# Attention then FFN on one core: FFN-only steps between the first two batches, range data sent once per batch, FFN spans that follow the attention chunks

## The chip, the core and the metric

One core of one Trainium2 chip runs one launch of the kernel. The metric is the device time of that launch in microseconds (us); less is better. The engines are named as the profile names them: PE (TensorE matmul), PEld (its weight load), DVE (VectorE), ACT (ScalarE), POOL (GpSimd), and SP, which here only issues transfers. SPq, ACTq and POOLq are the engines' instruction queues. Each engine works through its own instructions strictly in the order in which the program gives them, so an instruction that waits holds back all that stand behind it on that engine.

## What is computed

```python
def _attn_ref(q, k, v, beacon_k, beacon_v):          # q, k, v: (8, 8, 576, 64)
    k_all = np.concatenate([beacon_k, k], axis=2)     # 16 beacon rows in front: 592
    v_all = np.concatenate([beacon_v, v], axis=2)
    scores = scale * np.matmul(q, k_all.transpose(0, 1, 3, 2))
    scores = np.where(causal, -1e9, scores)           # beacons are always seen
    a = np.exp(scores - scores.max(-1, keepdims=True))
    a /= a.sum(-1, keepdims=True) + 1e-09
    return np.matmul(a, v_all)

def reference(**inputs):
    x = attn_out.transpose(0, 2, 1, 3).reshape(8 * 576, 512)
    return (np.maximum(x @ w_gate, 0) * (x @ w_val)) @ w_out   # 512 -> 1536 -> 512
```

## The kernel before, in words

Attention of 8 batches and 8 heads fills a matrix xT (512 x 4608, bf16, on chip); the FFN reads xT in tiles of 512 tokens. Both are cut into small pieces that a hand-written loop interleaves.

**Attention.** Heads go in 4 pairs per batch. A pair has 4 steps (i = 0 to 3), so a batch has 16. A step is `qk` (scores into PSUM tile s, 2 buffers), `softmax` (one exp on ACT, L270, then one or two masks on POOL, L273) and `av` (L293). Chunk 0 (tokens 0 to 240) is step 0; chunk 1 (240 to 496) is steps 1 and 2; chunk 2 (496 to 576) is step 3. At the last step of a chunk, `av` lets DVE take the reciprocal of the sums (L300, tile r) and multiply into xT (L302), and SP sends two rows of r to rsum (L304). At the end `count_in_range` looks at rsum on DVE (L348 to L352) and counts with one matmul (L354); every engine reads the count, and a general path that is not taken here hangs on it.

**FFN.** A group is either an up (L320 to L328: 4 matmuls with wg, relu on ACT, 4 matmuls with wv, a product on DVE into hT) or a down (L333: 12 matmuls, a copy on ACT, one store by SP). A whole tile is 12 ups and 4 downs. Ups and downs share the PSUM tile f (2 buffers).

**The loop.** It goes over a list of steps, two at a time; call one turn a pass. A pass issues `qk` of its two steps, then twice (softmax of one step, one FFN group from a queue if it holds any), then `av` of the two steps of the pass before. FFN groups come into the queue when the tokens of a span are ready; a span is a range of tokens. Spans before: 0 to 240, 240 to 512, then whole tiles. Batch 0 takes its steps chunk by chunk over all pairs; later batches take (1, 2) of each pair, then (0, 3) of each pair.

**Loading.** Batch 0 loads q and k as four wide tiles each and turns them on PE (L390 to L396, `turn_pair`, `turn_tail`). Each later batch has 15 units of 128 rows (k, q, v in turn, five row tiles t = 0 to 4). A unit is loaded by SP (L220) into one of the `stage` buffers (8), cast to bf16 by POOL (L238) and, for k and q, turned by a transfer that SP issues (L243) out of one of 6 `half` buffers. `fetch` puts the unit's load, cast and turn at steps of the batch before. In front of a pass's `qk` all that is due is issued: so POOL meets the casts of the next batch between the masks of the current one. The weights are loaded by POOL (L248): 8 quarters of wg and wv and one wo.

Of the kernel before, what the change touches and what calls it, by code (L numbers as in the profile page):

```python
# [146 lines left out]
def kernel(  # L147
# [38 lines left out]
    rsum = const.tile([2 * B * NP, S], FP32, name="rsum")  # L186
# [15 lines left out]
    class Batch:  # L202
        def __init__(self, b):
            self.b = b
            self.qT = kvq.tile([P, NP, S], BF16, name="qT")
            self.kT = kvq.tile([P, NP, NKT * P], BF16, name="kT")
            self.v = kvq.tile([P, NKT, d_model], BF16, name="v")
            self.raw, self.h = {}, {}
            nc.gpsimd.memset(self.kT[:, :, Stot:], 0.0)
# [69 lines left out]
    def av(pr, i):  # L279
# [18 lines left out]
        if i == last:  # L298
            r = nrm.tile([P, 256], FP32, name="r")
            nc.vector.reciprocal(r[:, :cn], o[:, 1, :cn])  # L300
            t0 = pr.batch.b * S + cq0
            nc.vector.tensor_mul(xT[:, pr.p, t0:t0 + cn], o[:, 0, :cn], r[:, :cn])  # L302
# [41 lines left out]
    def count_in_range():  # L344

        rows = 2 * B * NP
        ge = const.tile([rows, S], FP32, name="ge")
# [19 lines left out]
    with tc.manual_schedule():  # L367
# [5 lines left out]
        start = main.enter_context(tc.tile_pool(name="start", bufs=1))  # L373
# [3 lines left out]
        def load_pair(x, src, p, eng):  # L377
            t = wide[x, p] = start.tile([P, 2, 4 * D], FP32, name=f"wide_{x}{p}")
            eng.dma_start(t, src[0, 2 * p:2 * p + 2, :WIDE].rearrange("h (p r) d -> p h (r d)", r=4))

        def load_tail(x, src, beacon, eng):
            t = tails[x] = start.tile([P, d_model], FP32, name=f"tail_{x}")
# [5 lines left out]
        def turn_pair(x, p, copy):  # L388
            h = half.tile([P, 4, P], BF16, name="half")
            copy(h.rearrange("x r (h d) -> x h r d", d=D),  # L390
                 wide[x, p].rearrange("x h (r d) -> x h r d", d=D))
# [22 lines left out]
        load_tail("k", k, beacon_k[0], nc.sync)  # L414
        load_pair("q", q, 1, nc.scalar)
# [17 lines left out]
        for w in weights[:2]:  # L433
# [3 lines left out]
        later = {}  # L437
# [4 lines left out]
        for p in (2, 3):  # L442
            at(p - 1, lambda p=p: turn_pair("k", p, nc.vector.tensor_copy))
            at(p - 1, lambda p=p: turn_pair("q", p, nc.scalar.copy))
        at(3, lambda: turn_tail("q", nc.vector.tensor_copy))
        for t in range(2, NKT):
            at(t - 1, lambda t=t: b0.cast("v", t, nc.gpsimd.tensor_copy))
        for j, w in enumerate(weights[2:]):
            at(j // 2, w)

        def fetch(b, s0):
            at(s0, lambda: batches.append(Batch(b)))
            for j, u in enumerate(UNITS):
                s = s0 + j * 3 // 4
                at(s, lambda u=u: batches[b].load(*u))
                at(s + 2, lambda u=u: batches[b].cast(*u, nc.gpsimd.tensor_copy))
                if u[0] != "v":
                    at(s + 3, lambda u=u: batches[b].turn(*u))

        work, ready = [], {}  # L460
        for b in range(B):


            if b == 0:
                for c, (c0, cn, first, last) in enumerate(CHUNKS):
                    work += [(b, p, i) for p in range(NP) for i in range(first, last + 1)]
# [5 lines left out]
            if b + 1 < B:  # L472
                fetch(b + 1, 16 * b + (1 if b else 3))
# [67 lines left out]
```

## Time and profile before

| | |
|---|---|
| runs | 462.07 and 462.93 us, median 462.5 |
| the profiled execution | 461.52 us, of which the span from first to last instruction is 459.8 us |
| PE busy | 405.0 us (88%), 3545 matmuls |
| DVE, ACT, POOL busy | 243.9, 196.0 and 132.0 us |
| mean granted clock of PE | 0.967 of full speed |
| moved by DMA | 52.20 MB, mean 114 GB/s |

A row of a timeline has the start and the length in us, the engine, the line, the operation, what it writes <- what it reads, and in brackets how long the engine idled before it and what released it. PEclk is the granted clock of PE: 1.00 is 2.4 GHz, 0.50 is 1.2 GHz. MB in the DMA views agrees with packets times bytes in units of 2^20 bytes.

### The profile page before, as it was taken

How to read it: one execution, taken by the hardware profiler on the slowest of the kernel's cores; microseconds unless marked ns; L12 is line 12 of the kernel's file. 1: busy time of each engine (PE TensorE's matmuls, PEld its weight loads, DVE VectorE, ACT ScalarE, POOL GpSimd, SP SyncE). 2: the span in 40 equal slices, each digit the busy share in tenths (PEclk: the TensorE clock that was granted, in tenths of full speed). 3: DMA queues.
4: the chain of work that ended last, by engine and by line, in shares of the span. 5: the costliest groups of instructions: out<-in, count | busy, mean ns of one | idle time of the engine just before them, and what ended most of it. 6: DMA issues, size and time to landing. Idle time of an engine off the chain costs nothing.

```text
span 459.8 us, 9167 instructions
## 1 busy us (share of the span) xinstructions
PE 405.0 (88%) x3545; PEld 212.4 (46%) x3545; DVE 243.9 (53%) x330; ACT 196.0 (43%) x293; POOL 132.0 (29%) x293
## 2 busy tenths in 40 slices
PE   2547569869999999999999999999999997899994
PEld 1334345655454455544544554454545543344441
DVE  2544244655677466656755775577556755221320
ACT  2623235524554455445445554465355422122321
POOL 0931344242335224512442253234312100000000
PEclk9998699979999999999999999999999999799998
DMA  9999965893495449545944793568310010002002
GB/s 208 219 191 191 203 137 118 168 148 86 113 189 118 136 94 189 110 127 123 183 93 123 125 193 98 136 123 171 88 47 1 2 69 26 1 1 93 0 24 75
DMA packets 155011, 52.20 MB, mean 114 GB/s; under 512 B 142544, under 2 KB 150352, under 8 KB 154960
## 3 DMA queue, kind: packets, MB, share of 16 engines
q1 hardware_dynamic: 147568, 45.63, 48.3%
q0 software_dynamic: 5776, 4.72, 6.4%
q10 hardware_dynamic: 1616, 1.18, 1.0%
q8 instruction: 30, 0.49, 0.5%
q14 instruction: 21, 0.17, 0.1%
HBM read 38.27 MB, written 9.44 MB: 104 GB/s over the span
## 4 chain that ended last, share of the span: by engine, by line
PE 68%; DMA 13%; DVE 8%; SPq 3%; issue 3%; ACT 2%; POOL 1%; ACTq 0%; DVEq 0%; POOLq 0%
PE f L333 21%; PE f L326 18%; PE f L320 16%; PE o L293 8%; DMA raw<-in_v_dram 6%; DVE r L300 5%; PE s L262 4%; DMA raw<-in_k_dram 2%; SPq L243 2%; DMA raw<-in_q_dram 1%; ACT e L270 1%; DMA wide_k_131<-in_k_dram 1%; SPq L220 1%; DMA wide_q_120<-in_q_dram 1%; DVE hT L328 1%
## 5 line engine op out<-in xcount | busy, mean ns | idle before, releaser
L300 DVE RECIPROCAL r<-o 128x240 f32<-128x240 f32 (+2 forms) x96 | 129.9, 1353 | 71.4 <-PE o L293 63.9
L270 ACT ACTIVATE e<-s 128x736 bf16<-128x736 f32 (+3 forms) x128 | 110.1, 863 | 108.7 <-PE s L262 106.8
L328 DVE TENSOR_TENSOR hT<-g,f 128x512 bf16<-128x512 f32 (+2 forms) x120 | 75.9, 633 | 112.7 <-PE f L326 107.8
L320 PE MATMUL f<-xT,wg 128*128 128x512 bf16 (+2 forms) x480 | 120.7, 374 | 11.1 <-DVE xT L302 9.4
L326 PE MATMUL f<-xT,wv 128*128 128x512 bf16 (+2 forms) x480 | 117.0, 368 | 6.2 <-ACT g L323 3.3
L323 ACT ACTIVATE g<-f 128x512 f32<-128x512 f32 (+2 forms) x120 | 66.5, 554 | 72.5 <-PE f L320 71.4
L333 PE MATMUL f<-wo,hT 128*128 128x512 bf16 x432 | 96.2, 379 | 0.0
L326 PEld LDWEIGHTS <-wv 128*128 128x128 bf16 x480 | 48.3, 101 | 76.4 <-issue 36.9
L273 POOL TENSOR_SCALAR_AFFINE_SELECT e<-e 128x256 bf16<-128x256 bf16 (+2 forms) x160 | 57.3, 387 | 88.6 <-ACT e L270 88.6
L293 PE MATMUL o<-e,v 128*64 128x80 bf16 (+4 forms) x704 | 58.8, 241 | 13.6 <-POOL e L273 13.6
L238 POOL CAST half<-raw 128x512 bf16<-128x512 f32 (+1 forms) x70 | 42.7, 611 | 94.9 <-DMA raw<-in_q_dram 59.0
L320 PEld LDWEIGHTS <-wg 128*128 128x128 bf16 x480 | 44.8, 102 | 48.5 <-issue 8.8
L333 PEld LDWEIGHTS <-hT 128*128 128x128 bf16 x432 | 41.1, 98 | 49.2 <-issue 1.3
L293 PEld LDWEIGHTS <-v 128*64 128x64 bf16 (+1 forms) x704 | 37.5, 113 | 39.6 <-issue 37.4
L293 PE MATMUL o<-e,ones 128*64 128x80 bf16 (+4 forms) x704 | 53.7, 236 | 0.0
L336 ACT COPY ob<-f 128x512 f32<-128x512 f32 x36 | 21.1, 585 | 65.5 <-PE f L333 56.5
L238 POOL CAST v<-raw 128x512 bf16<-128x512 f32 (+1 forms) x40 | 24.6, 615 | 56.8 <-DMA raw<-in_v_dram 54.4
L262 PE MATMUL s<-qT,kT 64*128 64x80 bf16 (+3 forms) x704 | 37.1, 239 | 2.6 <-DMA rsum<-r 2.6
L293 PEld LDWEIGHTS <-ones 128*64 128x64 bf16 (+1 forms) x704 | 36.1, 114 | 0.1
L302 DVE TENSOR_TENSOR xT<-o,r 128x240 bf16<-128x240 f32 (+2 forms) x96 | 34.3, 358 | 3.3
L262 PEld LDWEIGHTS <-kT 64*128 64x128 bf16 x704 | 22.8, 98 | 9.6 <-issue 4.1
L394 PE MATMUL f<-ident,half 128*128 128x128 bf16 x32 | 4.5, 309 | 10.2 <-DVE half L390 9.2
(36 smaller groups left out, 30.1 us busy)
## 6 DMA issues: line engine op xcount, KB each, us to landing
out_dram<-ob SPq DMA_DIRECT2D x36, 256.0 KB
raw<-in_q_dram SPq DMA_DIRECT2D x28, 256.0 KB
raw<-in_v_dram SPq DMA_DIRECT2D x24, 256.0 KB
raw<-in_k_dram SPq DMA_DIRECT2D x21, 256.0 KB
raw<-in_v_dram SPq DMA_DIRECT2D x8, 224.0 KB
raw<-in_k_dram SPq DMA_DIRECT2D x7, 224.0 KB
wg<-in_moe_w_gate_dram POOLq DMA_DIRECT2D x4, 384.0 KB, 11.8
wv<-in_moe_w_val_dram POOLq DMA_DIRECT2D x4, 384.0 KB, 13.7
```

The costliest lines, as they stand in the source:

```text
L238: copy(dst, self.raw[x, t][:n])
L262: nc.tensor.matmul(s[:, a, c:c + n], pr.batch.kT[rows, pr.p, kt * P:(kt + 1) * P], pr.batch.qT[rows, pr.p, q0:q0 + n], start=True, stop=True)
L270: nc.scalar.activation(e[:, :, :n], pr.s[i][:, :, :n], AF.Exp, scale=scale)
L273: nc.gpsimd.affine_select(out=e[:, :, c:c + m], in_=e[:, :, c:c + m], pattern=[[0, 2], [1, m]], compare_op=ALU.is_ge, fill=0.0, base=base, ...
L293: nc.tensor.matmul(o[rows, part, q0 - cq0:q0 - cq0 + n], w, e[:kr, a, c:c + n], start=(i == first and j == 0 and part == 0), stop=(i == la ...
L300: nc.vector.reciprocal(r[:, :cn], o[:, 1, :cn])
L302: nc.vector.tensor_mul(xT[:, pr.p, t0:t0 + cn], o[:, 0, :cn], r[:, :cn])
L320: nc.tensor.matmul(g[:, :n], wg[:, ki, nf * P:(nf + 1) * P], x[:, ki], start=(ki == 0), stop=(ki == KM - 1))
L323: nc.scalar.activation(gs[:, :n], g[:, :n], AF.Relu)
L326: nc.tensor.matmul(u[:, :n], wv[:, ki, nf * P:(nf + 1) * P], x[:, ki], start=(ki == 0), stop=(ki == KM - 1))
L328: nc.vector.tensor_mul(self.h[:, nf, c0:c1], gs[:, :n], u[:, :n])
L333: nc.tensor.matmul(o, self.h[:, nf, ms * P:(ms + 1) * P], wo[:, nf, :], start=(nf == 0), stop=(nf == NF - 1))
```

## The change

It does five things. (1) Between the 16 steps of batch 0 and those of batch 1 stand 8 empty steps: a pass over them issues no attention, but goes on taking FFN groups from the queue. (2) The 15 loads of batch 1 are given out from step 6 on, its casts and turns only from step 16 on, that is in the empty steps; batches 2 to 7 keep the old spacing, one step earlier. (3) Batch 1 also goes chunk by chunk, and the second tile's span is cut at token 816, where batch 1's chunk 0 ends, so that tile has 12 ups of 304 columns and 12 of 208 instead of 12 of 512. (4) r becomes one tile per batch (128 x 4 x 576), and SP sends its two rows once per batch; rsum is 16 x 2304 instead of 64 x 576. (5) In the start, q pairs 2 and 3 and the q tail are loaded by SP instead of ACT, all staging goes through the `stage` buffers (11 of them), and the order of the weights and turns is new. What is issued at a step is split in two: `ahead` before `qk`, `later` between the two `qk` and the softmax.

```diff
-    rsum = const.tile([2 * B * NP, S], FP32, name="rsum")
+    rsum = const.tile([2 * B, NP * S], FP32, name="rsum")
...
-    stage = main.enter_context(tc.tile_pool(name="stage", bufs=8))
+    stage = main.enter_context(tc.tile_pool(name="stage", bufs=11))
...
-    nrm = main.enter_context(tc.tile_pool(name="nrm", bufs=3))
+    nrm = main.enter_context(tc.tile_pool(name="nrm", bufs=2))
...
+            self.r = nrm.tile([P, NP, S], FP32, name="r")
...
-            r = nrm.tile([P, 256], FP32, name="r")
-            nc.vector.reciprocal(r[:, :cn], o[:, 1, :cn])
...
-            g = 2 * (pr.batch.b * NP + pr.p)
-            nc.sync.dma_start(rsum[g:g + 2, cq0:cq0 + cn],
-                              r.rearrange("(a x) n -> a x n", a=2)[:, 0, :cn])
+            batch = pr.batch
+            r = batch.r[:, pr.p, cq0:cq0 + cn]
+            nc.vector.reciprocal(r, o[:, 1, :cn])
...
+            batch.chunks += 1
+            if batch.chunks == NP * len(CHUNKS):
+                nc.sync.dma_start(
+                    rsum[2 * batch.b:2 * batch.b + 2],
+                    batch.r.rearrange("(a x) p s -> a x (p s)", a=2)[:, 0])
...
-        rows = 2 * B * NP
-        ge = const.tile([rows, S], FP32, name="ge")
+        rows = 2 * B
+        ge = nrm.tile([rows, NP * S], FP32, name="r")
...
-        load_pair("k", k, 1, nc.sync)
-        for p in (2, 3):
-            load_pair("q", q, p, nc.scalar)
-        load_tail("q", q, None, nc.scalar)
         for t in range(2):
             b0.load("v", t)
         for p in (2, 3):
             load_pair("k", k, p, nc.sync)
+            load_pair("q", q, p, nc.sync)
+        load_tail("q", q, None, nc.sync)
...
-        for w in weights[:2]:
+        for w in weights[:4]:
             w()
...
+        ahead[2] = [lambda x=x, p=p, c=c: turn_pair(x, p, c) for p in (2, 3)
+                    for x, c in (("k", nc.vector.tensor_copy), ("q", nc.scalar.copy))]
+        ahead[4] = [lambda: turn_tail("q", nc.vector.tensor_copy)]
+        for w in weights[4:6]:
+            at(2, w)
+        at(2, lambda: b0.cast("v", 2, nc.gpsimd.tensor_copy))
+        for w in weights[6:]:
+            at(4, w)
+        for t in (3, 4):
+            at(4, lambda t=t: b0.cast("v", t, nc.gpsimd.tensor_copy))
...
+        GAP = 8
...
-            if b == 0:
+            if b < 2:
...
+            if b == 0:
+                work += [None] * GAP
+        fetch(1, lambda j: 6 + j // 2, lambda j: 16 + j // 2, lambda j: 16 + j // 2)
+        for b in range(2, B):
+            s0 = 16 * (b - 1) + GAP
+            fetch(b, lambda j, s0=s0: s0 + j * 3 // 4, lambda j, s0=s0: s0 + 2 + j * 3 // 4,
+                  lambda j, s0=s0: s0 + 3 + j * 3 // 4)
...
-        spans = [(0, 240), (240, 512)] + [(m, m + M_TILE) for m in range(M_TILE, n_tokens, M_TILE)]
+        spans = [(0, 240), (240, 512), (512, 816), (816, 1024)]
+        spans += [(m, m + M_TILE) for m in range(1024, n_tokens, M_TILE)]
```

POOL, late in batch 0: `e` is a mask, `half` and `v` are casts of batch 1 (L238), which wait for a transfer (DMAHW). This is the kernel before.

```order
38 L238 CAST half<-raw 128x512 [waits DMAHW0_49]
39 L273 AFFINE_SELECT e<-e 128x2x128 [waits PE_49,Activation_49]
40 L273 AFFINE_SELECT e<-e 128x2x128
41 L238 CAST half<-raw 128x512 [waits DMAHW5_49,DVE_49]
42 L238 CAST v<-raw 128x512 [waits DMAHW6_49]
43 L238 CAST half<-raw 128x512 [waits DMAHW7_49]
44 L273 AFFINE_SELECT e<-e 128x2x128 [waits PE_49,Activation_49]
```

The same engine and place after the change.

```order
39 L274 AFFINE_SELECT e<-e 128x2x128 [waits PE_49,Activation_49]
40 L274 AFFINE_SELECT e<-e 128x2x128
41 L274 AFFINE_SELECT e<-e 128x2x80 [waits Activation_49]
42 L274 AFFINE_SELECT e<-e 128x2x80 [waits PE_49,Activation_49]
43 L274 AFFINE_SELECT e<-e 128x2x80 [waits Activation_49]
44 L274 AFFINE_SELECT e<-e 128x2x80 [waits PE_49,Activation_49]
45 L239 CAST half<-raw 128x512 [waits DMAHW2_49,DMAHW1_49]
46 L239 CAST half<-raw 128x512 [waits DMAHW3_49,DVE_49]
47 L239 CAST v<-raw 128x512 [waits DMAHW5_49,DMAHW4_49]
```

Before, masks of batch 0 stand behind casts of batch 1; after, all 15 casts of batch 1 (rows 45 to 59) stand behind the last mask of batch 0 and ahead of the first mask of batch 1 (row 61).

SP at the end of batch 1's loads, after the change: rows 29 to 32 are the last four loads of batch 1, each of which waits for a cast on POOL to give a stage buffer back; DMA_TRANSPOSE is a turn.

```order
28 L221 DMA raw<-in_q_dram 128x8x64 [waits DMAHW5_49,Pool_49]
29 L221 DMA raw<-in_v_dram 128x8x64 [waits DMAHW6_49,Pool_49]
30 L221 DMA raw<-in_k_dram 80x8x64 [waits DMAHW7_49,Pool_49]
31 L221 DMA raw<-in_q_dram 64x8x64 [waits DMAHW0_49,Pool_49]
32 L221 DMA raw<-in_v_dram 80x8x64 [waits DMAHW1_49,Pool_49]
33 L244 DMA_TRANSPOSE kT<-half 128x4x128 [waits DMAHW2_49]
34 L244 DMA_TRANSPOSE qT<-half 128x4x128 [waits DMAHW3_49]
35 L244 DMA_TRANSPOSE kT<-half 128x4x128 [waits DMAHW4_49]
36 L307 DMA rsum<-r 2x2304 [waits DMAHW5_49,DVE_49]
37 L244 DMA_TRANSPOSE qT<-half 128x4x128 [waits DMAHW6_49,Pool_49]
```

Before, SP had the turns of batch 1 between its loads, and up to twelve rsum transfers of batch 0 among them:

```order
20 L220 DMA raw<-in_k_dram 128x8x64 [waits DMAHW0_49,Pool_49]
21 L304 DMA rsum<-r 2x240 [waits DMAHW1_49,DVE_49]
22 L304 DMA rsum<-r 2x240 [waits DMAHW2_49,DVE_49]
23 L243 DMA_TRANSPOSE kT<-half 128x4x128 [waits DMAHW3_49,Pool_49]
24 L243 DMA_TRANSPOSE qT<-half 128x4x128 [waits DMAHW4_49,Pool_49]
25 L220 DMA raw<-in_q_dram 128x8x64 [waits DMAHW5_49]
```

So all loads of batch 1 now stand ahead of its first turn, and one rsum transfer stands where twelve were.

## Rows read from the trace of the kernel before

**Rows 1.** The page, span in 40 slices of 11.5 us: PE busy, tenths.
```profile
PE   2547569869999999999999999999999997899994
```

**Rows 2.** Waits of PE, 0 to 67 us: total, times, longest (us).
```profile
PE o L293 <- POOL e L273: 10.7, 4, 5.0
...
PE f L320 <- DVE xT L302: 4.7, 1, 4.7
```

**Rows 3.** Timeline of POOL, 20 to 70 us.
```profile
50.37 0.61 POOL L238 CAST half<-raw 128x512 bf16<-128x512 f32 x1 [7.00 <-DMA raw<-in_q_dram]
```

**Rows 4.** Timeline of all engines, 20 to 60 us.
```profile
26.68 5.46 SPq L304 DMA_DIRECT2D rsum<-r  x2
29.98 1.66 DVE L300 RECIPROCAL r<-o 128x240 f32<-128x240 f32 x1 [2.98 <-DMA rsum<-r]
...
34.99 3.20 SPq L243 DMA_TRANSPOSE qT<-half  x1
```

**Rows 5.** Stretches: busy us (count) per engine, then PEclk, DMA share, GB/s.
```profile
0.00:10.00 10.00, 1.66 (x12) 0.95 (x12) 2.04 (x6) 3.00 (x4) 0.89 (x7) 1.00 0.87 206
...
50.00:60.00 10.00, 5.21 (x55) 3.81 (x55) 2.99 (x4) 2.31 (x4) 4.91 (x10) 0.66 1.10 189
...
393.00:399.00 6.00, 6.00 (x16) 2.12 (x16) 0.69 (x1) 1.19 (x2) 0.00 (x0) 0.53 0.01 1
```

**Rows 6.** DMA queues (packets, MB), 30 to 35 us, then 50 to 55 us.
```profile
q0 software_dynamic: 961, 0.71, 91.0%
q1 hardware_dynamic: 961, 0.24, 36.7%
...
q1 hardware_dynamic: 3846, 0.96, 111.2%
```

**Rows 7.** Timeline of PE: qk at the start of four passes.
```profile
67.05 0.56 PE L262 MATMUL s<-qT,kT 64*128 64x256 bf16 x8 [2.58 <-DMA rsum<-r]
...
77.10 0.56 PE L262 MATMUL s<-qT,kT 64*128 64x256 bf16 x8
...
81.27 0.56 PE L262 MATMUL s<-qT,kT 64*128 64x256 bf16 x8
...
108.08 0.56 PE L262 MATMUL s<-qT,kT 64*128 64x256 bf16 x8
```

**Rows 8.** Timeline of DVE in the pass from 81.27 us.
```profile
81.38 1.76 DVE L300 RECIPROCAL r<-o 128x256 f32<-128x256 f32 x1 [0.38 <-PE o L293]
...
83.51 0.43 DVE L328 TENSOR_TENSOR hT<-g,f 128x272 bf16<-128x272 f32 x1
```

**Rows 9.** Groups by form: busy us, mean ns.
```profile
L300 DVE RECIPROCAL r<-o 128x240 f32<-128x240 f32 x32 | 52.9, 1654 | 54.4 <-PE o L293 51.5 <-DMA rsum<-r 3.0
...
L300 DVE RECIPROCAL r<-o 128x80 f32<-128x80 f32 x32 | 20.7, 648 | 0.1
```

**Rows 10.** The chain that ended last: start, length, what.
```profile
114.40 1.67 DVE r L300
...
158.80 1.67 DVE r L300
...
235.25 5.29 PE f L333 x24
...
241.82 5.29 PE f L333 x24
```

**Rows 11.** Timeline, 382 to 393 us: the count.
```profile
382.43 0.38 PE L320 MATMUL f<-xT,wg 128*128 128x512 bf16 x1 [1.08 <-DVE xT L302]
...
389.99 0.45 DVE L348 TENSOR_SCALAR ge<-rsum 64x576 f32<-64x576 f32 x1
390.47 0.75 DVE L349 SCALAR_TENSOR_TENSOR ge<-rsum,ge 64x576 f32<-64x576 f32 x1
...
392.06 0.16 PE L354 MATMUL o<-ones,ok 64*1 64x1 bf16 x1 [2.78 <-DVE ok L352]
...
392.96 1.86 PE L320 MATMUL f<-xT,wg 128*128 128x512 bf16 x4 [0.74 <-DVE cnt L356]
```

More of the change, by code (lines that the diff above doesn't have):

```diff
@@ L372 @@
         rest = S - WIDE
-        start = main.enter_context(tc.tile_pool(name="start", bufs=1))
         tails = {}
@@ L377, in load_pair @@
         def load_pair(x, src, p, eng):
-            t = wide[x, p] = start.tile([P, 2, 4 * D], FP32, name=f"wide_{x}{p}")
-            eng.dma_start(t, src[0, 2 * p:2 * p + 2, :WIDE].rearrange("h (p r) d -> p h (r d)", r=4))
+            t = wide[x, p] = stage.tile([P, d_model], FP32, name="raw")
+            eng.dma_start(t.rearrange("p (h e) -> p h e", h=2), src[0, 2 * p:2 * p + 2, :WIDE].rearrange("h (p r) d -> p h (r d)", r=4))
         def load_tail(x, src, beacon, eng):
-            t = tails[x] = start.tile([P, d_model], FP32, name=f"tail_{x}")
+            t = tails[x] = stage.tile([P, d_model], FP32, name="raw")
             for p0, a in ((0, src[0, :, WIDE:]), (rest, beacon)):
@@ L432, with fetch @@
         b0.cast("v", 1, nc.gpsimd.tensor_copy)
-        for w in weights[:2]:
+        for w in weights[:4]:
             w()
-        later = {}
+        ahead, later = {}, {}
         def at(step, action):
             later.setdefault(step, []).append(action)
[L442 to L452, printed above, removed]
+        ahead[2] = [lambda x=x, p=p, c=c: turn_pair(x, p, c) for p in (2, 3)
[8 more added lines that the diff above has]
+            at(4, lambda t=t: b0.cast("v", t, nc.gpsimd.tensor_copy))
+        def fetch(b, load, cast, turn):
+            at(load(0), lambda: batches.append(Batch(b)))
             for j, u in enumerate(UNITS):
-                s = s0 + j * 3 // 4
-                at(s, lambda u=u: batches[b].load(*u))
-                at(s + 2, lambda u=u: batches[b].cast(*u, nc.gpsimd.tensor_copy))
+                at(load(j), lambda u=u: batches[b].load(*u))
+                at(cast(j), lambda u=u: batches[b].cast(*u, nc.gpsimd.tensor_copy))
                 if u[0] != "v":
-                    at(s + 3, lambda u=u: batches[b].turn(*u))
+                    at(turn(j), lambda u=u: batches[b].turn(*u))
+        GAP = 8
         work, ready = [], {}
         for b in range(B):
-            if b == 0:
-                for c, (c0, cn, first, last) in enumerate(CHUNKS):
-                    work += [(b, p, i) for p in range(NP) for i in range(first, last + 1)]
+            if b < 2:
+                for c, (c0, cn, lo, hi) in enumerate(CHUNKS):
+                    work += [(b, p, i) for p in range(NP) for i in range(lo, hi + 1)]
                     ready[len(work)] = b * S + c0 + cn
@@ L481 @@
             while spans and spans[0][1] <= have:
-                t0, t1 = spans.pop(0)
-                f = ffn_tiles[t0 // M_TILE]
-                c0, c1 = t0 - f.m0, t1 - f.m0
-                queue += f.groups(c0, c1, c0 // P, c1 // P)
+                add_ffn()
             now = [s for s in range(s0, s0 + STRIDE) if s < len(work)]
             for s in now:
-                for act in later.pop(s, []):
+                for act in ahead.get(s, []):
                     act()
-                b, p, i = work[s]
-                qk(pairs.setdefault((b, p), Pair(batches[b], p)), i)
+                if work[s]:
+                    b, p, i = work[s]
+                    qk(pairs.setdefault((b, p), Pair(batches[b], p)), i)
             for j in range(STRIDE):
                 if j < len(now):
-                    b, p, i = work[now[j]]
-                    softmax(pairs[b, p], i)
+                    for act in later.pop(now[j], []):
+                        act()
+                    if work[now[j]]:
+                        b, p, i = work[now[j]]
+                        softmax(pairs[b, p], i)
                 if queue:
@@ L498 @@
             for s in range(s0 - STRIDE, s0):
-                if 0 <= s < len(work):
+                if 0 <= s < len(work) and work[s]:
                     b, p, i = work[s]
                     av(pairs[b, p], i)
-        for t0, _ in spans:
-            queue += ffn_tiles[t0 // M_TILE].groups(0, M_TILE, 0, M_TILE // P)
+        while spans:
+            add_ffn()
         for j, g in enumerate(queue):
@@ L508 @@
     main.close()
-    with tc.If(in_range < 2 * B * NP):
+    with tc.If(in_range < 2 * B):
         general_path(tc, q, k, v, beacon_k, beacon_v, out, ident, wg, wv, wo)
```

16 lines of the change are left out of this document (10 added, 6 removed).

## The prediction, made before the changed kernel ran

> **What bounds the kernel now.** I read the page's slices first, then the waits of PE, then the timelines of the engines that PE waits for, and last the DMA queues. The slices [rows 1] show two kernels. From slice 11 (about 115 us) PE is busy 9 tenths or more until the end, except around slices 34 and 35. Before that it is half idle. So a change in the steady part can only pay by taking PE work away; a change in the first 108 us can pay by letting PE work earlier. There PE waits longest for masks on POOL (10.7 us in four waits) and once 4.7 us for xT [rows 2]. POOL itself was not busy: it stood in front of a cast of batch 1, up to 7.00 us, for a transfer to land [rows 3], and the masks of batch 0 stood behind that cast. The wait for xT has its own cause: a reciprocal waited 2.98 us for an rsum transfer to give its r buffer back, on a queue where two such issues took 5.46 us [rows 4]. The transfers are the resource behind both: 206 GB/s in the first 10 us [rows 5]. While the weights flow on q0 they and SP's queue q1 move the same number of packets, but q1's packets are small: 0.24 MB in 5 us against 0.71, and 0.96 MB in 5 us once q1 is alone [rows 6].
>
> Two marks carry the sum: batch 1's first qk at 67.05 us and batch 2's first qk at 108.08 us [rows 7]. By the second one 26 FFN groups are done (one per step from step 6 to 31).
>
> **Part 1: when does batch 1 start?** Two bounds.
> Transfers: a batch is (576 + 592 + 592) x 512 x 4 bytes = 3.44 MB, two are 6.88, and batch 1's first qk needs 4 turns of 0.125 MB, together 7.4 MB on q1. The first 10 us move 2.06 MB [rows 5] and the next 2.5 us at that rate 0.5: 2.6 MB when the weights begin to flow. That I put at 12.5 us: they are issued behind the cast of v's second tile, which has less ahead of it than before. (Should they flow 3.5 us later, q1 has 0.7 MB more by then, and the end hardly moves.) The weights are 4.5 MB, at 0.71 MB per 5 us 32 us [rows 6]; q1 moves 1.5 MB beside them. At 44.5 us q1 has 4.1 of 7.4 MB; 3.3 MB at 0.96 MB per 5 us are 17 us: 61.5 us, with landing 63. The turns are queued behind all loads, so the full 7.4 MB counts.
> Work: v's last tiles of batch 0 now land beside the weights. After the first 2.6 MB there are about 0.9 MB left, at 0.24 MB per 5 us some 18 us, so near 31 us; their casts stand ahead of the masks of step 4, and av of steps 4 and 5 comes at 33 us. Up to there I count no gain. From then on batch 0 meets no cast of batch 1. Five passes at 4.17 us (77.10 to 81.27, with ups of 272 columns, [rows 7]) end at 54 us. The six groups of the remaining three empty passes are one down at 2.65 us (24 matmuls in 5.29, [rows 10]) and five ups at about 1.2 us, 8.6 us: 62.5 us. Casts start at about 50 us, after the last mask of batch 0; the last four loads wait for the first four casts, and q1 still has 1.3 MB in flight then, so it doesn't run dry.
> Both bounds say 63 us, and 24 - 6 = 18 groups are done, where before it was 67 us and 10 groups.
>
> **Part 2: from there to batch 2.** DVE's order prices a pass with small groups: after av it takes reciprocal, product into xT, and only then the product of the first up, from 81.38 to 83.94 us [rows 8]; the second up's wv matmuls need that f buffer. So a pass is 2.6 + 0.2 (start and release) + 0.5 (4 matmuls, 0.22 us each at 512 columns, [rows 10]) + 0.85 (av, the rest of the 4.17) = 4.2 us, almost whatever the columns, as long as PE has less than that to do. Batch 1's eight passes (steps 24 to 39) hold 7 ups of 272, 3 downs and 6 ups of 304: no av before it 2.9; then 3.7; behind two chunk-0 reciprocals (1.65 each, [rows 9], and their products, 0.4 each, 83.14 to 83.51 in [rows 8]) 5.5; an up and a down 5.0; two downs 6.55 (235.25 to 241.82, [rows 10]); 4.2, 4.2 and 4.0. Sum 36 us (bounds: 30, PE's own work, and 41, as before): batch 2 starts at 99 us instead of 108.1, that is -9.0, with 34 groups done instead of 26.
>
> **Part 3: the rest of the loop.** It is 48 passes and a last one in both kernels. A steady batch takes 158.80 - 114.40 = 44.4 us [rows 10]: two down passes of 6.55 and six up passes of 5.2. Before, the rest holds 36 up and 13 down passes; after, 30 up, 10 down and 9 with ups of 304 or 208 columns, DVE's bound again: 2.9 us behind the av with steps 0 and 3 (1.65 + 0.65, [rows 9], and two products, 0.6), so 4.25. That is -6 x 5.2 - 3 x 6.55 + 9 x 4.25 = -12.6 us, though PE's own work in those nine is only about 3 us each. The twelve additional groups push four downs behind the loop, +10.5 us: -2.1 us together. These light passes ask for as many loads as the others in less time; I add 2 us of waits for transfers (bounds 0 and, at 0.6 us a pass, 6).
>
> **Part 4: the count.** Before, PE lost 1.08 us for the last xT, then 2.78 + 0.16 + 0.74 = 3.7 us around the count [rows 11], then 6 us at a clock of 0.53 [rows 5], which lose 2.8 us: 7.6 us. After, the four downs (10.5 us) need no xT of the last batch and stand ahead of the count, so the xT wait goes. What is late next is DVE: its three instructions have 2304 columns instead of 576, on 16 rows. From 0.45, 0.75 and about 0.75 us at 576 columns [rows 11] I take 4 times the part that grows (all but 0.15): 1.35 + 2.55 + 2.55 = 6.45 us (bounds: unchanged 1.95, four times everything 7.8). The last reciprocal ends 2.5 us after the last av, the rsum transfer needs about 2 us, the three 6.45, the matmul and the copy 0.9: PE goes on 11.9 us after the last av, the downs end at 10.5. I take 1.4 us of idle and no loss of clock (bounds: a gain of 1.9 and a price of 4 more): -6.2 us.
> One rule speaks against this part. In the Trainium skill, "DMA: Bandwidth & Descriptors", section on why a DMA increments its semaphore by 16, a transfer uses the largest number of engines up to 16 that divides its slowest dimension, hence two for the two rows of r, which are now 9.2 KB each. No run here shows how many engines it uses. By it the transfer takes an estimated 0.7 us longer (a sixteenth of the rate per engine), and the forecast would be 0.7 us higher.
>
> **The other edits.** The rsum transfers leave SP's queue, 11 of 12 per batch; in the steady part PE waits for none, so there they are worth 0; in the start their gain is in part 1. Loading q pairs by SP instead of ACT is before the weights flow: 0 (bounds -1 and +3, should the weights catch the last pair). `stage` with 11 buffers: its waits are the four loads named above.
>
> **Sum.** 459.8 - 9.0 - 2.1 + 2 - 6.2 = 444.5 us of span. The profiled execution took 1.7 us more than its span and 1.0 us less than the median of the runs, so 446.2 us as such an execution, 447 us as a median.
>
> **Rivals.**
> A. Batch 1's preparation takes the place of the waits removed: casts and turns begin only when batch 0's last mask is through, and the ten turns go one behind the other at the 3.2 us that a turn took beside the weights [rows 4], 32 us where I count on them in the shadow of 24 us of passes. For: SP's order, where all turns stand behind all loads. Against: the weights are through by then. It moves batch 2's start by 8 us: 455 us.
> B. The light passes cost 5 us and not 4.2, because POOL there waits for transfers as it did in batch 1 before. For: such waits are what POOL had most of [rows 3]. Of seventeen passes twelve at 0.8 us: 9.6 us, 456 us.
> C. Slower than before. In the light passes PE idles 1 to 1.4 us in each, at DVE's product. In the stretch from 50 to 60 us the clock was 0.66 while PE was half idle [rows 5]; if it is granted at 1.2 GHz in these passes too, PE's 3 to 3.5 us become 6 to 7, past DVE's 4.2 us, from which point it decides. At 2.3 us for each of 17 passes that is 39 us: 486 us; with half of them 467 us. Against: the passes from 77.10 us on were of the same kind and ran at the 4.17 us that I use [rows 7].
> D. No waits for transfers (2 us), and the nine light passes at 3.45 us, nearer to PE's own 3 (7 us): 447 - 2 - 7 = 438 us.
>
> **How the numbers follow.** Forecast 0.60, A 0.15, B 0.10, C 0.05, D 0.10. Faster by over 2% (about what a measurement of this kernel can tell from no change) is below 453.3 us: forecast, D and a few hundredths less for the forecast's upper edge, 0.67. Within 2%: A, B and that edge, 0.27. Slower: 0.06, C and a little more. The range leaves out C and half of D: 439 to 457 us.
>
> **What would show it.** Right: no wait of POOL for a transfer between masks of batch 0; batch 1's qk (two steps of 240 columns) near 63 us and batch 2's near 99; up passes of 4.2 us with 304 and 208 columns, released by DVE; four downs before the count and an idle PE of 1 to 2 us there. Wrong: batch 1's qk after 70 us; av of step 4 well after 33 us (weights ahead of v's tiles); a clock below 1.00 between 70 and 150 us; a count that takes over 4 us.

## The result, and the profile after

The changed kernel took 449.09 us (448.45 and 449.73) where the kernel before took 462.5: a ratio of 0.971, 95% interval 0.9639 to 0.9781. Its profiled execution had a span of 446.7 us; the forecast was 447 us for the median and 444.5 for the span. A later job, in which the changed kernel ran four times and the kernel before fourteen, gives a smaller gain: 451.41 against 460.23 us, ratio 0.9803 (0.9771 to 0.9835). The first job shows a gain of over 2%; the later one leaves it open whether it is above or below 2%.

The page's slices answer to [rows 1]; a slice is 11.2 us here. The second row is the granted clock.

```profile
PE   3588875999987999999999999999999998999994
...
PEclk9999989899999999999999999999999999999999
```

Slices 3 to 6 have 8, 8, 8 and 7 where before they had 4, 7, 5 and 6, and the dip near the end has shrunk to one digit. A new hole stands in slice 7 (67 to 78 us), with a clock below full on both sides of it.

The waits of PE over the whole span (total, times, longest, us) answer to [rows 2].

```profile
PE f L330 <- DVE hT L332: 8.2, 22, 1.0
...
PE o L294 <- POOL e L274: 4.3, 2, 3.8
...
PE s L263 <- DMA qT<-half: 2.3, 1, 2.3
PE f L324 <- DVE xT L304: 1.9, 2, 1.7
```

Before, PE waited 10.7 us for masks up to 67 us and 13.6 over the whole span; now it is 4.3 over the whole span, all of it after 67 us. Of the wait of 4.7 us for xT 1.7 are left. The wait that comes most often, 22 times and up to 1.0 us, is for DVE's product hT, which the prediction named as the release of its light passes. Where masks are waited for is seen in PE's timeline, which answers to [rows 7] (start, length, tile, and in brackets the idle time before and what ended it):

```profile
62.72 0.49 PE L263 MATMUL s<-qT,kT 64*128 64x240 bf16 x8 [2.28 <-DMA qT<-half]
66.22 0.80 PE L263 MATMUL s<-qT,kT 64*128 64x240 bf16 x8
70.10 0.56 PE L263 MATMUL s<-qT,kT 64*128 64x256 bf16 x8
...
77.45 0.39 PE L294 MATMUL o<-e,v 128*64 128x240 bf16 x2 [3.76 <-POOL e L274]
...
79.51 0.93 PE L263 MATMUL s<-qT,kT 64*128 64x256 bf16 x8
...
104.70 0.56 PE L263 MATMUL s<-qT,kT 64*128 64x256 bf16 x8
```

62.72 us is batch 1's first qk (67.05 before), 104.70 batch 2's (108.08 before). The pass from 70.10 took 9.41 us; in it PE stood 3.76 us for a mask. POOL's timeline, which answers to [rows 3], has the reason:

```profile
46.91 1.17 POOL L239 CAST half<-raw 128x512 bf16<-128x512 f32 x2
...
75.34 0.61 POOL L239 CAST half<-raw 128x512 bf16<-128x512 f32 x1 [9.64 <-DMA raw<-in_k_dram]
76.46 0.61 POOL L239 CAST half<-raw 128x512 bf16<-128x512 f32 x1 [0.51 <-DMA raw<-in_beacon_v_dram]
77.02 0.74 POOL L274 TENSOR_SCALAR_AFFINE_SELECT e<-e 128x224 bf16<-128x224 bf16 x2
```

Batch 1's casts begin at 46.91, behind the last mask of batch 0: the mishap of [rows 3] is cured for batch 0. At 75.34 it has come back one batch later: a cast of batch 2 waits for its load, and batch 1's masks (77.02) stand behind it. The load was late, because SP issues it behind ten turns of batch 1, of which the first and the last are:

```profile
55.30 1.39 SPq L244 DMA_TRANSPOSE kT<-half  x1
...
69.67 1.19 SPq L244 DMA_TRANSPOSE qT<-half  x1
70.90 0.58 SPq L221 DMA_DIRECT2D raw<-in_beacon_k_dram  x1
```

PE also works at a lower clock here. Stretches, as in [rows 5]:

```profile
60.00:70.00 10.00, 7.70 (x68) 4.90 (x66) 2.22 (x6) 4.51 (x9) 5.02 (x11) 0.83 0.62 116
70.00:80.00 10.00, 4.99 (x52) 3.36 (x50) 6.30 (x8) 2.41 (x4) 3.77 (x8) 0.88 0.77 141
80.00:90.00 10.00, 9.87 (x68) 5.11 (x67) 4.89 (x6) 5.03 (x7) 4.44 (x9) 0.95 1.14 196
```

The 0.83 of the first row is older than the stall: it comes behind the wait of 2.28 us for a turn at 62.72 us (0.73 from 62 to 66 us, 1.00 again from 70 to 74). The 0.88 and 0.95 come behind the stall (0.69 from 76 to 80 us).

The end, as in [rows 11], is the timeline of all engines:

```profile
362.18 10.54 PE L337 MATMUL f<-wo,hT 128*128 128x512 bf16 x47
...
364.85 0.52 SPq L307 DMA_DIRECT2D rsum<-r  x1
...
367.15 1.35 DVE L352 TENSOR_SCALAR r<-rsum 16x2304 f32<-16x2304 f32 x1 [2.06 <-DMA rsum<-r]
...
368.54 2.54 DVE L353 SCALAR_TENSOR_TENSOR r<-rsum,r 16x2304 f32<-16x2304 f32 x1
...
371.12 2.54 DVE L356 TENSOR_REDUCE ok<-r 16x1 bf16<-16x2304 f32 x1
...
373.72 0.16 PE L358 MATMUL o<-ones,ok 16*1 16x1 bf16 x1 [1.00 <-DVE ok L356]
...
374.94 1.02 PE L324 MATMUL f<-xT,wg 128*128 128x512 bf16 x4 [1.06 <-DVE cnt L360]
```

Four down groups (47 matmul records) run from the last av on, while DVE counts beside them. The next group starts 12.76 us after the last av, 2.2 us after the downs (1.00 + 0.16 + 1.06), in this execution at full clock: four matmuls take 1.02 us, where before they took 1.86.

### The profile page after: what moved, and what is told of

Same layout as the page of the kernel before. It is cut to its first block, busy times and chain, and to the rows that moved or that the text cites. A ratio compares the mean times of both kernels' runs of the same rounds, so it can differ in the third digit from the quotient of the medians.

```text
span 446.7 us, 9136 instructions
## 1 busy us (share of the span) xinstructions
PE 397.7 (89%) x3591; PEld 217.4 (49%) x3641; DVE 247.7 (55%) x342; ACT 196.2 (44%) x305; POOL 131.2 (29%) x293
## 4 chain that ended last, share of the span: by engine, by line
PE 62%; DVE 17%; issue 6%; ACT 5%; DMA 4%; SPq 3%; POOL 2%; DVEq 0%; ACTq 0%; POOLq 0%
PE f L337 18%; PE f L330 17%; PE f L324 13%; DVE r L302 9%; PE o L294 9%; DVE hT L332 5%; PE s L263 4%; ACT e L271 3%; SPq L244 2%; DVE xT L304 1%; ACT g L327 1%; DMA raw<-in_q_dram 1%; DMA raw<-in_beacon_k_dram 1%; POOL e L274 1%; DMA raw<-in_beacon_v_dram 1%
## 5 line engine op out<-in xcount | busy, mean ns | idle before, releaser
L332 DVE TENSOR_TENSOR hT<-g,f 128x512 bf16<-128x512 f32 (+4 forms) x132 | 77.5, 588 | 106.3 <-PE f L330 102.9
L330 PE MATMUL f<-xT,wv 128*128 128x512 bf16 (+4 forms) x511 | 115.1, 342 | 15.0 <-DVE hT L332 8.2
L324 PE MATMUL f<-xT,wg 128*128 128x512 bf16 (+4 forms) x511 | 116.6, 345 | 6.9 <-ACT g L327 2.7
L327 ACT ACTIVATE g<-f 128x512 f32<-128x512 f32 (+4 forms) x132 | 68.6, 519 | 63.6 <-PE f L324 61.7
L337 PE MATMUL f<-wo,hT 128*128 128x512 bf16 x416 | 95.2, 380 | 0.9
L274 POOL TENSOR_SCALAR_AFFINE_SELECT e<-e 128x256 bf16<-128x256 bf16 (+2 forms) x160 | 58.2, 386 | 114.4 <-ACT e L271 110.3
L330 PEld LDWEIGHTS <-wv 128*128 128x128 bf16 x528 | 51.5, 98 | 70.5 <-issue 33.6
L324 PEld LDWEIGHTS <-wg 128*128 128x128 bf16 x528 | 47.8, 99 | 49.0 <-issue 11.9
L294 PE MATMUL o<-e,ones 128*64 128x80 bf16 (+4 forms) x704 | 52.8, 235 | 0.0
L294 PEld LDWEIGHTS <-v 128*64 128x64 bf16 (+1 forms) x704 | 36.0, 112 | 27.4 <-issue 26.7
```

What stands on the lines that cost most here:

```text
L274: nc.gpsimd.affine_select(out=e[:, :, c:c + m], in_=e[:, :, c:c + m], pattern=[[0, 2], [1, m]], compare_op=ALU.is_ge, fill=0.0, base=base, ...
L294: nc.tensor.matmul(o[rows, part, q0 - cq0:q0 - cq0 + n], w, e[:kr, a, c:c + n], start=(i == first and j == 0 and part == 0), stop=(i == la ...
L324: nc.tensor.matmul(g[:, :n], wg[:, ki, nf * P:(nf + 1) * P], x[:, ki], start=(ki == 0), stop=(ki == KM - 1))
L327: nc.scalar.activation(gs[:, :n], g[:, :n], AF.Relu)
L330: nc.tensor.matmul(u[:, :n], wv[:, ki, nf * P:(nf + 1) * P], x[:, ki], start=(ki == 0), stop=(ki == KM - 1))
L332: nc.vector.tensor_mul(self.h[:, nf, c0:c1], gs[:, :n], u[:, :n])
```

## The experiments

Twelve kernels ran, in three jobs and a last one of a single kernel. Times are medians; ratios are against the kernel before on the same chip in the same job. "Tail" is the time from the end of the last av to the end of the span, in the profiled execution.

| kernel | us | ratio (95%) | first qk of batch 1, 2 | tail |
|---|---|---|---|---|
| the changed kernel again | 451.41 | 0.9803 (0.9771 to 0.9835) | 63.35, 105.91 | 85.8 |
| rsum alone | 457.50 | 0.9950 (0.9916 to 0.9985) | 66.28, 100.94 | 83.0 |
| early casts | 458.99 | 0.9995 (0.9968 to 1.0022) | 80.58, 116.29 | 84.3 |
| batch 2's casts 4 steps later | 447.52 | 0.9723 (0.9695 to 0.9751) | 63.27, 103.06 | 84.4 |
| no split | 460.12 | 1.0014 (0.9980 to 1.0048) | 69.49, 105.37 | 82.5 |
| twelve steps | 454.49 | 0.9872 (0.9819 to 0.9925) | 64.50, 105.57 | 82.6 |
| batch 2's casts 2 steps later | 446.08 | 0.9692 (0.9642 to 0.9743) | 63.65, 101.40 | 85.8 |
| short count | 450.15 | 0.9799 (0.9744 to 0.9853) | 64.08, 106.21 | 83.0 |
| four steps | 464.61 | 1.0133 (1.0074 to 1.0193) | 63.04, 104.48 | 100.5 |
| twelve steps, late count | 443.63 | 0.9668 (0.9609 to 0.9727) | 64.19, 105.14 | 73.8 |
| 2 steps later, late count | 443.53 | 0.9672 (0.9614 to 0.9729) | 63.49, 101.69 | 82.9 |
| all three | 442.81 | 0.9638 (0.9599 to 0.9677) | 64.22, 104.37 | 73.8 |

**The changed kernel again**, without an edit. 

> The changed kernel itself, beside the others on the same chip, so that they can be compared with it. Expected 449 us, ratio to the kernel before 0.97. Every theory expects the same.

The pass behind 70.67 us has the same wait for POOL, 3.55 us: the stall is no accident of one execution. The full clock behind the count was one. Here PE stood just as long, and four matmuls then took up to 1.91 us (timeline of PE); the granted clock from 376 to 382 us was 0.72, and the tail is 85.8 us where the first execution has 84.5:

```profile
376.39 1.48 PE L324 MATMUL f<-xT,wg 128*128 128x512 bf16 x4 [1.05 <-DVE cnt L360]
377.66 1.91 PE L330 MATMUL f<-xT,wv 128*128 128x512 bf16 x4
```

**The one transfer of r alone**, in the kernel before:

```diff
-    rsum = const.tile([2 * B * NP, S], FP32, name="rsum")
+    rsum = const.tile([2 * B, NP * S], FP32, name="rsum")
...
+            if batch.chunks == NP * len(CHUNKS):
+                nc.sync.dma_start(
+                    rsum[2 * batch.b:2 * batch.b + 2],
+                    batch.r.rearrange("(a x) p s -> a x (p s)", a=2)[:, 0])
```

> Part 4 alone on the kernel before: r is one tile per batch and range data goes once per batch; nothing else is moved (two start tiles and the two tails lie in buffers of the FFN that are free then, so that r fits). Theory (the gain of the change is the order of casts and masks on POOL plus the empty steps): the wait of the third reciprocal for its buffer (3.0 us) and the 4.7 us wait for xT near 32 us go, but POOL still waits for batch 1's loads, so batch 1's first qk moves from 67 to some 64 us at best; the count costs about 4.5 us more, since its three DVE instructions take 6.4 us instead of 1.95 with no downs ahead of them. Sum -3 + 4.5: 464 us, the same as before. Rival (the twelve small transfers per batch on SP's queue were the brake): batch 1's first qk at 60 us or earlier, 455 us or less.

457.50 us lies between the two: 2.7 us less than the kernel before in the same job, where the theory had 1.5 us more and the rival some 7.5 less. Neither had batch 1's start right (66.28). Its timeline, of POOL and of PE:

```profile
51.06 0.61 POOL L239 CAST half<-raw 128x512 bf16<-128x512 f32 x1 [7.21 <-DMA raw<-in_q_dram]
...
389.79 0.16 PE L358 MATMUL o<-ones,ok 16*1 16x1 bf16 x1 [7.27 <-DVE ok L356]
```

Batch 1 starts only 0.8 us earlier than before (66.28), since POOL's stall is still there. But its eight passes then take 34.7 us (66.28 to 100.94), where before they took 41.0. Most of the difference lies in the passes from 85.44 us on in the kernel before: there PE stood for a mask behind casts of the next batch, and the granted clock from 90 to 100 us was 0.74. PE's timeline of the kernel before:

```profile
96.11 0.41 PE L293 MATMUL o<-e,v 128*64 128x240 bf16 x2 [2.50 <-POOL e L273]
```

With the one transfer no such wait is left in these passes, and the clock is 1.00 from 60 to 110 us. How the fewer transfers brought the next batch's loads in time was not tested. The longer count takes 4.5 us of that back (7.27 against 2.78 us). The theory had the second term and not the first.

**Batch 1's casts from step 8, turns from step 9**, in the changed kernel:

```diff
-        fetch(1, lambda j: 6 + j // 2, lambda j: 16 + j // 2, lambda j: 16 + j // 2)
+        fetch(1, lambda j: 6 + j // 2, lambda j: 8 + j // 2, lambda j: 9 + j // 2)
```

> The changed kernel with one part undone: batch 1's casts are due from step 8 on and its turns from step 9 on, so they stand among batch 0's masks on POOL and among the loads on SP again; the empty steps stay. Theory: batch 0's masks wait for batch 1's transfers again, batch 0's last av comes 13 to 16 us later (near 65 us instead of 51), the empty passes come after it, batch 1's first qk near 74 us instead of 62.7; some of it is given back because batch 2's loads are ready earlier: 455 to 460 us. Rival (the empty steps alone make the gain, wherever the casts stand, since the transfers set when batch 1 can start): qk near 63 to 65 us, 449 us.

The theory held for the time: the whole gain is gone (ratio 0.9995). Batch 1's first qk came later than it said, at 80.58 us and not near 74. PE waits 16.8 us for masks, at worst here:

```profile
49.04 0.42 PE L294 MATMUL o<-e,v 128*64 128x256 bf16 x2 [9.76 <-POOL e L274]
```

So the eight FFN-only steps pay nothing as soon as casts of batch 1 stand ahead of batch 0's masks.

**Batch 2's casts and turns four steps later**, then two:

```diff
-            fetch(b, lambda j, s0=s0: s0 + j * 3 // 4, lambda j, s0=s0: s0 + 2 + j * 3 // 4,
-                  lambda j, s0=s0: s0 + 3 + j * 3 // 4)
+            d = 6 if b == 2 else 2
+            fetch(b, lambda j, s0=s0: s0 + j * 3 // 4, lambda j, s0=s0, d=d: s0 + d + j * 3 // 4,
+                  lambda j, s0=s0, d=d: s0 + d + 1 + j * 3 // 4)
```

> The changed kernel with batch 2's casts due 4 steps later (turns too); its loads are where they were. Theory for the 5.7 us by which batch 2's start was later than forecast: batch 2's first casts stand ahead of batch 1's masks of its third step on POOL, and their loads were issued behind batch 1's ten turns, so av waited 3.8 and 0.5 us and the clock fell. Then the wait of PE for POOL near 77 us goes, batch 2's first qk moves from 104.7 to about 99.5 us, and the time to 444 us. Rival (the data is late whatever the order, and the wait only moves): the wait comes back at later casts or at batch 2's first qk, 449 us; if the turns then end too late for batch 2, slower, 451 us.

447.52 us is between the theory and the rival. With d = 6 PE waits only 0.2 us for masks, but the turns are now late at batch 2, as the rival had it:

```profile
103.06 0.56 PE L263 MATMUL s<-qT,kT 64*128 64x256 bf16 x8 [2.80 <-DMA qT<-half]
```

With d = 4:

> The changed kernel with batch 2's casts and turns two steps later than it has them (half of the delay of the run with four steps). Theory (POOL's casts of batch 2 stand in front of masks of batch 1 by 3.8 us, and a delay of four steps gave about 3 us and then lost 2.8 us for a late turn): with two steps the mask's wait is mostly gone and the turn is in time: 445 to 447 us, lower than with four steps. Rival (what is won at the one place is lost at the other in any case, because the transfers of batch 2 end when they end): 448 to 450 us, and batch 2's first qk no earlier than 103 us.

```profile
71.80 0.56 PE L263 MATMUL s<-qT,kT 64*128 64x256 bf16 x8
...
76.29 0.56 PE L263 MATMUL s<-qT,kT 64*128 64x256 bf16 x8
...
101.40 0.56 PE L263 MATMUL s<-qT,kT 64*128 64x256 bf16 x8
```

The pass that took 9.41 us takes 4.49, batch 1 takes 37.75 us instead of 41.98, and batch 2's qk waits for no turn: theory. In time, 446.08 us is 5.3 us below the changed kernel's 451.41 and 3.0 below its first 449.09, but these are different jobs; the 4.2 us of the two traces are the safer figure.

**No split:** batch 1 in the old order of steps, one span for tokens 512 to 1023.

```diff
-            if b < 2:
+            if b == 0:
...
-        spans = [(0, 240), (240, 512), (512, 816), (816, 1024)]
-        spans += [(m, m + M_TILE) for m in range(1024, n_tokens, M_TILE)]
+        spans = [(0, 240), (240, 512)] + [(m, m + M_TILE) for m in range(M_TILE, n_tokens, M_TILE)]
```

> The changed kernel, but batch 1 in the old order of steps (both middle steps of every pair first, then the outer ones), and tokens 512 to 1023 as one FFN span: it has no spans that follow batch 1's chunks. The eight FFN-only steps, the early preparation and the one transfer of r per batch stay. Theory (what the split pays is cover for the count: its twelve additional groups push four down groups behind the loop, while the loop itself gains little from its light passes): for want of groups the queue is empty for some eight slots, so four attention-only passes of about 3.3 us stand in the loop and it ends within 3 us of the changed kernel's, but at the end the groups behind the loop need the last batch's xT at once and PE waits there for DVE's chain (about 7 us with the long instructions of the count): 453 to 457 us. Rival (the split makes batches 1 and 2 run faster of itself, as the prediction's light passes of 4.25 us against 5.2 and 6.55 us have it): the loop is over 8 us longer as well, 460 us or more. A second rival, that the split is worth nothing: 449 to 451 us.

460.12 us, above the theory's range, at the rival's edge. But the loop is not over 8 us longer, as the rival had it: the last av ends 14.0 us later (376.2 against 362.2), with four more downs, 10.5 us, done by then. That leaves 3.5 us for the loop. Two places, both in PE's timeline:

```profile
69.49 0.93 PE L263 MATMUL s<-qT,kT 64*128 64x256 bf16 x8 [9.65 <-DMA qT<-half]
...
392.16 0.16 PE L358 MATMUL o<-ones,ok 16*1 16x1 bf16 x1 [7.27 <-DVE ok L356]
```

The second is the count without cover: the tail is 82.5 us with no down group left over, where the changed kernel's 84.5 less its four downs (10.5) is 74.0: 8.5 us. The first was in neither theory: the old order's first qk reads columns up to 496, and so waits for more turns than the new order's, which reads 240. Following the chunks lets batch 1 start 6.8 us earlier (62.72 against 69.49), of which the 3.5 us are left at the end of the loop. With the 8.5 us at the count that is the whole difference of the two spans, 12.0 us: most of what the split pays is cover, as the theory had it.

**Twelve FFN-only steps, and four:**

```diff
-        GAP = 8
+        GAP = 12
```

> The changed kernel with twelve FFN-only steps between the first two batches and not eight: two more passes of two FFN groups each stand ahead of batch 1. Theory (the start of batch 1 is set by the transfers and turns, which reach it at about 63 us whatever stands before, and then POOL's casts of batch 2 stop batch 1's masks, since their loads are issued behind ten turns): batch 1's first qk comes at about 67.5 us with no wait for a transfer and four more groups done, the wait of 2.3 us and most of POOL's 3.8 us go, and fewer groups stand behind the loop: 444 to 447 us. Rival (FFN groups are the same work wherever they stand, and what is done early leaves light passes later in which PE idles at DVE's product): batch 1 starts later by what the groups take and nothing comes back: 449 to 452 us.

A miss: 454.49. Batch 1 starts with no wait for a transfer (64.50), but the loop has taken all four down groups, and the count stands bare again; then PE's clock falls. PE's timeline, then the stretch:

```profile
387.47 0.16 PE L358 MATMUL o<-ones,ok 16*1 16x1 bf16 x1 [7.27 <-DVE ok L356]
388.37 1.87 PE L324 MATMUL f<-xT,wg 128*128 128x512 bf16 x4 [0.74 <-DVE cnt L360]
```

```profile
388.00:394.00 6.00, 5.63 (x16) 2.11 (x16) 0.69 (x1) 1.19 (x2) 0.00 (x0) 0.60 0.02 5
```

With `GAP = 4`:

> The changed kernel with four FFN-only steps between the first two batches and not eight. Theory (batch 1 starts when its turns have landed, at 62 to 64 us, whatever stands ahead, so the FFN-only steps are work that PE does in a time in which it would otherwise wait): batch 1's first qk stays within 2 us of the changed kernel's, PE waits 6 to 11 us for a turn there, and four more groups stand behind the loop: 452 to 458 us. Rival (the steps only shift the same work, and the gain comes from the early preparation alone): batch 1 starts some 4 us earlier and the time stays at 449 to 451 us.

464.61 us: the start came as the theory had it, the time did not. Timelines of PE and of DVE:

```profile
63.04 0.80 PE L263 MATMUL s<-qT,kT 64*128 64x240 bf16 x8 [8.04 <-DMA qT<-half]
...
377.29 0.16 PE L358 MATMUL o<-ones,ok 16*1 16x1 bf16 x1 [7.26 <-DVE ok L356]
```

```profile
370.14 0.69 DVE L332 TENSOR_TENSOR hT<-g,f 128x512 bf16<-128x512 f32 x1 [1.18 <-PE f L330]
370.74 1.34 DVE L352 TENSOR_SCALAR r<-rsum 16x2304 f32<-16x2304 f32 x1
```

Batch 1 starts within 0.4 us of the changed kernel's with half the steps: its start is set by the turns, and the steps fill time in which PE would wait. Eight groups are left behind the loop, but the first four are ups. The count stands behind four groups by its place in the program, DVE works in order, and so its first instruction starts only behind the fourth up's product. Cover is not a number of groups but groups without work for DVE. Tail 100.5 us, 16 more: four ups at 1.87 us, and 8.5 for the count.

**The count on 64 rows of 576 columns**, two transfers per batch:

```diff
-                nc.sync.dma_start(
-                    rsum[2 * batch.b:2 * batch.b + 2],
-                    batch.r.rearrange("(a x) p s -> a x (p s)", a=2)[:, 0])
+                g = 2 * NP * batch.b
+                for a in range(2):
+                    nc.sync.dma_start(rsum[g + NP * a:g + NP * (a + 1)],
+                                      batch.r[a * D:a * D + 1])
```

> The changed kernel with its range data laid out on 64 rows of 576 columns again, by two transfers per batch, still once per batch: DVE's three instructions of the count are a quarter as long, at the same place behind four down groups. Theory (the count's three instructions of 6.4 us end the chain from the last av to the next matmul of the FFN, 12.8 us against 10.5 us of cover): the chain is 8 to 8.5 us, the idle time of PE at the count, 2.2 us, goes, and the time falls by 1.5 to 2.5 us: 446.5 to 447.5 us where the changed kernel has 449. Rival (the transfer or the sequence of the last FFN tile sets the end, not the count): no change, within 0.7 us of the changed kernel.

The idle time at the count went, and what is left is PE's wait for the last down's copy (timeline of DVE, then of PE):

```profile
369.06 0.45 DVE L353 TENSOR_SCALAR r<-rsum 64x576 f32<-64x576 f32 x1 [2.39 <-DMA rsum<-r]
...
370.33 0.75 DVE L357 TENSOR_REDUCE ok<-r 64x1 bf16<-64x576 f32 x1
```

```profile
375.12 1.02 PE L325 MATMUL f<-xT,wg 128*128 128x512 bf16 x4 [0.74 <-ACT ob L341]
```

PE goes on 11.3 us after the last av instead of 12.76, but the ratio, 0.9799, is that of the changed kernel. A term of 1.5 us is below what these runs resolve: the trace shows PE going on earlier, and no run shows that it pays.

**The count at the end**, with twelve steps:

```diff
-            if j == 4:
-                in_range = count_in_range()
+            if j == len(queue) - 4:
+                ok = count_in_range()
+            if j == len(queue) - 1:
+                in_range = count_rows(ok)
```

(`count_rows` holds the matmul and the copy, which stood at the end of `count_in_range`.) 

> The run with twelve FFN-only steps again, with the count's three DVE instructions put ahead of the last four down groups, and its matmul and copy ahead of the very last one. Theory (with twelve steps the loop itself got no worse; what was lost is the cover: no down group is left over behind the loop, so PE waited 7.3 us for the count and then ran matmuls at half the clock): that loss of 8 to 11 us goes: 444 to 447 us. Rival (twelve steps cost time in the loop, the count has no part in it): 451 us or more.

443.63 us against 454.49: the miss of the twelve steps was the cover, and the tail says it (82.6 to 73.8). PE's timeline and the stretches from 80 us show something else:

```profile
82.34 0.41 PE L324 MATMUL f<-xT,wg 128*128 128x304 bf16 x1 [1.72 <-DVE xT L304]
82.55 1.22 PE L330 MATMUL f<-xT,wv 128*128 128x304 bf16 x4
...
88.75 0.68 PE L330 MATMUL f<-xT,wv 128*128 128x304 bf16 x4
```

```profile
80.00:84.00 4.00, 2.17 (x10) 1.14 (x9) 2.38 (x4) 1.96 (x3) 0.56 (x1) 0.68 1.15 282
84.00:88.00 4.00, 4.00 (x32) 2.46 (x29) 1.35 (x3) 0.42 (x1) 1.99 (x5) 0.50 1.21 194
```

Behind a wait of 1.72 us for DVE's xT, four matmuls of 304 columns take 1.22 us, and 0.68 from 88 us on. As an estimate from these rows, some 2.5 us (half of 82.5 to 87.4) are still to be had there.

**Two steps later with the late count**, then all three together. 

> The changed kernel with batch 2's casts and turns two steps later, as in the run that did this alone, and with the count at the end of the program as in the run before this one (three DVE instructions ahead of the last four down groups, matmul and copy ahead of the last). Theory (the two losses are separate: POOL's casts in front of batch 1's masks, and the idle 2.2 us of PE at the count): the gains add up, and the time is 2 to 2.5 us below that of the late casts alone: 443 to 444.5 us. Rival (the count's idle time is made up elsewhere, as it was with the shorter instructions): 445.5 to 446.5 us.

443.53 us is in the theory's range; the tail is 82.9 against 85.8 us. 1.3 us of that are the clock behind the count, which fell in the profiled execution of the late casts alone as in the changed kernel again, and the ratios of the two runs (0.9672 and 0.9692) can't be told apart. The late count was not run by itself. 

> All three together: twelve FFN-only steps, batch 2's casts and turns two steps later, and the count's instructions among the last four down groups. Theory (POOL's masks behind casts still cost PE 2.3 us with twelve steps, and the late casts take that away, while the start has no wait for a turn): 441 to 442.5 us. Rival (twelve steps and late casts remove the same wait, so they don't add up): 443 to 444.5 us, as with either alone.

442.81 us lies between the two ranges; against either pair the difference is within the intervals. Against the changed kernel run again it is not: 0.9638 (0.9599 to 0.9677) and 0.9803 (0.9771 to 0.9835), some 7.5 us. The interval of the changed kernel's first measurement (0.9639 to 0.9781) still touches it.

## Why the prediction was right, and where it was not

The forecast's time was right, in part by luck: two errors nearly cancel. Of the span's 2.2 us more than forecast, part 1 gave -0.3, part 2 +6.0, part 3 -4.3 and part 4 +0.8.

Part 1 was right. 63 us was said for batch 1's first qk, by transfers and by work alike; it came at 62.72. Which of the two bounds held was left open; the rows and the runs say transfers: a wait of 2.28 us for a turn, 8.04 us with four steps, none with twelve, and a start between 62.7 and 64.5 each time. v's last tile was cast at 23.6 us and not near 31, which made the work end about 2 us earlier and changed nothing.

Part 2 is where it failed. Eight passes were to take 36 us and took 41.98. The step at fault is the price of the third pass, 5.5 us, for which only DVE's two reciprocals were counted. It took 9.41 us, because a cast of batch 2 stood ahead of batch 1's masks, and the next one 5.81 us, where 5.0 was said, at a clock below 1.00. The first pass took 3.50 us and not 2.9, at the clock that had fallen behind the wait for the turn. The prediction spoke of such waits under rival B, but as 0.8 us on twelve passes, not as one stall behind ten turns; with the casts two steps later the eight passes take 37.75 us. A clock below 1.00 between 70 and 150 us, named as a sign of error, was there (0.88 and 0.95), from this stall and not from the light passes as in rival C: with the casts two steps later both stretches have 1.00.

Part 3 was too dear. Batch 2's first qk came 5.7 us later than forecast, yet the last av ended only 1.4 us later than the forecast implies (362.2 against 444.5 less a tail of 83.7, the measured 84.5 without the 0.8 us more of idle time at the count): the rest of the loop was 4.3 us cheaper. The 2 us of waits for transfers did not come, and nine light passes took 35.6 us (3.7 to 4.3 each) and not 9 x 4.25 = 38.25. Rival D had both terms with the right sign.

Part 4 was right in its mechanism and close in size. From the last av to the next group: 2.67 us to the transfer's issue (2.5 said), 2.30 to DVE's first instruction (2), 6.51 for the three (6.45), 1.28 for matmul, copy and release (0.9), together 12.76 (11.9). PE went on 2.2 us after the downs against 1.4. "No loss of clock" was true of this execution and not of the next, which lost 1.3 us. The runs with four and twelve steps and with no split show what it hung on: with the count where it is, exactly four downs, no ups, left over behind the loop. The 0.7 us that, by the prediction's estimate, the Trainium skill's rule on the number of engines ("DMA: Bandwidth & Descriptors", section on why a DMA increments its semaphore by 16) would have added for two long rows can't be seen: two transfers with eight shorter rows in all let DVE wait 2.39 us, the one with two rows 2.06. No run shows how many engines either used.

Of the other edits, the one transfer of r was not worth 0 outside the start. Alone in the kernel before it brought 6.4 us in batch 1's passes. How much of that lies in the changed kernel's time can't be told apart, as no run had the change without it.

Rival A had the right queue and the wrong victim. The ten turns took 15.6 us from the first issue to the next load (55.30 to 70.90) and not 32, so batch 1 waited only 2.28 us for one; but what stands behind them, batch 2's loads, was late. No run put these loads ahead of the turns. The run with early casts shows the other side: with casts eight steps earlier and turns seven, the preparation costs the whole gain.

## What to carry to other kernels

An engine that works in order turns a late transfer into a stall of whatever stands behind the instruction that waits for it. When such a stall is cured for one stage, look for the next stage's first load and for what is queued ahead of it: here a delay of two steps there gave 4.2 us in batch 1's passes. Cover for a chain at the end must be work that leaves the chain's engine free: four down groups hid 10.5 us of the chain from the last av to the count, and four up groups, with a product on DVE in each, hid none of DVE's three instructions.

## What the runs showed that was not expected

Short idle times cost a second time through the clock, but not in every execution. At the count, five profiled executions have the same rows: 10.5 us of unbroken matmuls, then 2.2 us until the next group. In three of them (the changed kernel's first, early casts, batch 2's casts 4 steps later) the clock stayed at 1.00, four matmuls took 1.02 us, and the tails are 84.3 to 84.5 us. In two (the changed kernel again, 2 steps later) it fell, to 0.72 over 6 us, four matmuls took up to 1.91 us, and the tails are 85.8 us. What decided between them is not shown. Elsewhere, a wait of 1.72 us at 80 us was followed by a stretch at 0.50, the level of 1.2 GHz, and a wait of 7.27 us at the count by 0.60 over 6 us.

Batch 1's start moved by less than 2 us, 62.72 to 64.50, in ten profiled executions with four, eight or twelve FFN-only steps ahead of it (all but those with early casts and with no split, which change its preparation or its order): up to eight PE waits there for a turn, and with twelve PE's own work reaches the same point.
